# Threshold attention, then a GELU layer pair: the first batch's weights turned in TensorE's transpose mode, divided afterwards

## The chip, the cores and the metric

The kernel runs on one core of a Trainium2 chip. A core has a matrix engine (TensorE, PE in the profile), three engines for elementwise work (VectorE, DVE; ScalarE, ACT; GpSimd, POOL), a queue that only issues transfers (SyncE, SP) and 16 DMA engines. The engines run at the same time, each through its own list of instructions in order, and wait for each other by semaphores. The metric is the device time of one execution in microseconds; the lower, the better. Matmul results land in PSUM, small accumulation memory that TensorE writes and VectorE and ScalarE read; everything else lies in SBUF.

## What is computed

```python
# q, k, v: (8, 8, 576, 64) float32; tau = 0.02
scores = (q @ k.T) / sqrt(64)                       # per batch and head: 576 x 576
scores = where(scores >= max(scores, -1) - tau, scores, -1e9)
attn = exp(scores - max(scores, -1))
attn = attn / (sum(attn, -1) + 1e-9)
x = (attn @ v) -> (8 * 576, 8 * 64)                 # tokens x 512
h = x @ w_in                                        # 512 x 2048, float64 in memory
out = (0.5 * h * (1 + erf(h / sqrt(2)))) @ w_out    # 2048 x 512, float64 in memory
```

Eight batches of eight heads; then a feed-forward pair over all 4608 tokens. The matrix weights arrive as float64.

## The kernel before

**Work and its order.** The order of all instructions is written out by hand. Two heads make a pair (`p`), four pairs a batch (HP = 4), 32 pairs in all. A pair's 576 queries are cut into four chunks of 128 (two heads each) and one tail of 64 per head, both tails in one chunk: five steps (p, i). The main loop goes through steps, numbered n. In the first batch (p < EARLY = 4) n = 0 to 7 are the chunks 0 and 1 of the four pairs, n = 8 to 19 the chunks 2, 3 and the tail of each; from n = 20 on (BATCH) whole pairs follow one another. Each step issues, in this order: the scores (L403) and the head of the softmax (maximum L415 on VectorE, threshold L416 on GpSimd, exponential L418 on ScalarE); the product with v of an earlier step, where one is due; some work of the feed-forward blocks; the turning of the weights of the step before; the tail of the softmax (mask and sum, L434 on VectorE, then 1e-9 added to the sums, L437 on GpSimd).

**Turning.** The product with v needs the attention weights p with the keys on the partitions, so each 128 x 576 block of p is turned. From the second batch on VectorE turns blocks of 32 and DMA regroups them; x^T is then divided by the sums on GpSimd (`divide`, L545), with inverse sums that a DMA spreads over the partitions (`divisors`). In the first batch TensorE turns (`turn_p_early`, L335): `diagonal` (L440) takes the inverse of each query's sum on VectorE (L445) and ScalarE scales a 128 x 128 identity by it, for each of the two heads (L448); a matmul of p with that diagonal (L345) turns a block and divides it at once. A full step has ten: four blocks of 128 for each head, and two tails of 64 keys, one above the other. ScalarE copies the results out of PSUM (L353, L357, L364). In the first batch p is laid out so that the 64 tail keys of the first head and those of the second stand side by side.

**Product with v.** `weigh_v` (L506) makes x^T of a pair, 64 partitions for each head, and ScalarE copies it to its place in `xall` (L531), blocks of 256 tokens. In the first batch it is due after chunk 1 of a pair (tokens 0 to 255) and after its tail (256 to 575): `due` in the main loop.

**Weights.** The matrices come as 32 pieces of 128 x 512 float64. GpSimd's queue loads each twice, once as it is (L186) and once shifted by three bytes (L188); a generator `conversions` issues VectorE's and ScalarE's instructions that make float32 of them (L207, L208, L215, L217, L220), a few in each step, and each finished piece lets the next load go.

**Feed-forward.** 18 blocks of 256 tokens. The first eight are worked off between the attention steps, piece by piece: 64 matmuls of the first layer (L597), copies or gelus on ScalarE (L564, L570), 32 of the second (L612). `GOAL` says how many blocks are to be done by which step n; `goal` interpolates, `fill` issues what is owed. In the first batch the gelus are held back (the first layer's results are only copied, L564) and done together at n = 20 (`gelus_held`), because they need another function table than the exponentials (ACT_TABLE_LOAD). The last ten blocks follow in two groups of five after the attention, by a scheme with fewer products (L785, L667).

**PSUM.** Apart from the scores' two buffers, one pool of four banks (tag "mm") serves the turning (`tr`), x^T, the first layer (`hT`) and the second (`o_ps`). A bank is used again when its reader, mostly ScalarE, is done.

Of the kernel before, what the change touches and what calls it, by code (L numbers as in the profile page):

```python
# [18 lines left out]
def kernel(  # L19
# [40 lines left out]
    TAIL = S - MAIN  # L60
# [5 lines left out]
    TOK = 256  # L66
# [13 lines left out]
    ps = ctx.enter_context(tc.tile_pool(name="ps", bufs=4, space=PSUM))  # L80
# [12 lines left out]
    dg = late_end.enter_context(tc.tile_pool(name="dg", bufs=1))  # L93
    gp = late_end.enter_context(tc.tile_pool(name="gp", bufs=N_DF // 2 + 2))
    op = late_end.enter_context(tc.tile_pool(name="op", bufs=2))
# [25 lines left out]
    ident = const.tile([P, P], FP32, name="ident")  # L121
# [118 lines left out]
    st = {}  # L240
    x_blk = {}
# [93 lines left out]
    def turn_p_early(p, i):  # L335


        s = st[p]
        if i == 0 or (p < HP and i == 2):
            s["pT"] = [one.tile([P, KR, S], FP32, tag=f"pT{e}", name=f"pT{e}") for e in range(2)]  # L340
        w, diag = s.pop(("p", i)), s.pop(("diag", i))
        n = 1 if i == NC else 2

        def turn(to, cols, e):
            nc.tensor.matmul(to, lhsT=w[:, cols], rhs=diag[:, e, :], start=True, stop=True)  # L345

        for e in range(n):
            tr = ps.tile([P, NC, P], FP32, tag="mm", name="tr")
            for c in range(NC):
                at = e * (S + TAIL) + c * P  # L350
                turn(tr[:, c, :], slice(at, at + P), e)
            if i < NC:
                nc.scalar.copy(s["pT"][e][:, 0:NC, i * P:(i + 1) * P], tr)  # L353
        if i == NC:
            copy = nc.vector.tensor_copy if p == EARLY - 1 else nc.scalar.copy
            for e in range(2):
                copy(s["pT"][e][:, 0:NC, MAIN:S], tr[:, :, e * TAIL:(e + 1) * TAIL])  # L357
        tails = s["pT"][0][:, NC, :]
        tr = ps.tile([P, NC, P], FP32, tag="mm", name="tr")
        if i < NC:  # L360
            for e in range(2):
                at = MAIN + e * TAIL
                turn(tr[e * TAIL:(e + 1) * TAIL, 0, :], slice(at, at + TAIL), e)
            nc.scalar.copy(tails[:, i * P:(i + 1) * P], tr[:, 0, :])  # L364
            return
        turn(tr[0:TAIL, 0, :], slice(MAIN, S), 0)
        for e in range(2):
            rows = slice(e * TAIL, (e + 1) * TAIL)
            copy(tails[rows, MAIN:S], tr[0:TAIL, 0, rows])

    def scale_q(p):
        t = st[p]["q"]
# [64 lines left out]
            nc.gpsimd.tensor_scalar(pair[:, 0:n], pair[:, 0:n], 1e-9, None, op0=ALU.add)  # L437
            s["sum", i] = pair[:, 0:n]

    def diagonal(p, i):  # L440

        s = st[p]
        den = s.pop(("sum", i))
        n = den.shape[1]
        nc.vector.reciprocal(den, den)  # L445
        diag = s["diag", i] = dg.tile([P, 2, P], FP32, tag="inv", name="diag")
        for e in range(n):
            nc.scalar.activation(diag[:, e, :], ident, AF.Copy, bias=0.0, scale=den[:, e:e + 1])  # L448

    def divisors(p):  # L450

# [54 lines left out]
    def weigh_v(p, lo, hi):  # L506


        b, hp = divmod(p, HP)
        s = st[p]  # L510
        xT = ps.tile([P, 512], FP32, tag="mm", name="xT")
        for c in range(KR):
            for e in range(2):
                f = slice(e * D, (e + 1) * D)
                to = xT[f, 0:hi - lo]
                if p < EARLY:
                    rhs = s["pT"][0 if c == NC else e][:, c, lo:hi]
                else:
                    to = to.rearrange("p (g s) -> p g s", s=2 * Q)
                    rhs = by_64(s["pT"][e])[:, lo // (2 * Q):hi // (2 * Q), c, :]  # L520
                nc.tensor.matmul(  # L521
                    to, lhsT=s["v"][:, e, c, :], rhs=rhs, start=(c == 0), stop=(c == KR - 1))
        for n, o, at, size in in_blocks(b, lo, hi):
            if n not in x_blk:
                x_at[n] = x_slot(x_place(n))
                x_blk[n] = xall[:, x_at[n], :, :]
            to, x = x_blk[n][:, hp, o:o + size], xT[:, at - lo:at - lo + size]
            if p < EARLY and size == TOK:
                to = to.rearrange("q (p c) -> q c p", c=2)
                x = x.rearrange("q (c p) -> q c p", c=2)  # L530
            nc.scalar.copy(to, x)  # L531

    def in_blocks(b, lo, hi):
        while lo < hi:
            n, o = divmod(b * S + lo, TOK)
            size = min(TOK - o, hi - lo)
            yield n, o, lo, size
            lo += size
# [481 lines left out]
    BATCH = HP * SLOTS  # L1020
# [2 lines left out]
    DIVIDE = 3  # L1023
    START = 2 * HP + 2

    GOAL = [(-1, 0.0), (START - 1, 0.0), (BATCH - 1, 0.42)]
    GOAL += [(BATCH * (m + 2) + DIVIDE, x) for m, x in enumerate([1.92, 2.89, 3.86, 4.82, 5.79, 6.75])]
    GOAL += [(BATCH * B - 1, PLAIN - 0.44), (BATCH * B + 1, PLAIN - 0.17), (BATCH * B + WEIGH, PLAIN - 0.17)]

# [14 lines left out]
    for n in range(len(slots) + WEIGH + 1):  # L1044
        p, i = slots[n] if n < len(slots) else divmod(n, SLOTS)
        early = p < EARLY
        last = slots[n - 1] if 0 < n <= len(slots) else None
        if p < NP:
            scores(p, i)
            softmax_head(p, i)  # L1050
            if p < HP - 1 and i == 0:
                turn_qk_early(p + 1)
        elif n == len(slots):
            early_end.close()
            weights_first()
        gelus(0)
        if n == BATCH:
            gelus_held()
        table()
        for args in due:  # L1060
            weigh_v(*args)
        due = []
        if p > EARLY and i == WEIGH:
            for lo, hi in (0, WIDE), (WIDE, S):
                weigh_v(p - 1, lo, hi)
            if p == NP:
                divide(p - 1)
        owed += (goal(n) - goal(n - 1)) * BLK_NS * (PARTS[i] if not early and p < NP else 1.0)
        if early:
            fill(owed, tokens)  # L1070
            owed = 0.0
            table()
        if last and last[0] < EARLY and last[1] < NC:
            turn_p_early(*last)
        if early and n > 2:
            convert(0, 700 if i == NC else 1)
        if p < NP:
            softmax_tail(p, i)
        if p < NP and not early:
            turn_p(p, i)  # L1080
        if p < NP and not early:
            if i == 2:
                regroup(p, 1)
            if i > 2:
                regroup(p, i)
            if i == NC:
                divisors(p)
        if last and last[0] < EARLY and last[1] == NC:
            turn_p_early(*last)
        if p < 2 and i == 0:  # L1090
            load_piece()
            load_v_early(p + 2)
        if p == 1 and i == NC:
            load(HP)
        if n == BATCH - 3:
            load(HP + 1)
        if n == BATCH:
            for t in pd_tail + [turned_p[:, e, h, :, :] for e in range(2) for h in range(2)]:
                nc.gpsimd.memset(t[:, NB:4 * KR, :], 0.0)
        if EARLY < p < NP and i == DIVIDE:  # L1100
            divide(p - 1)
        if p >= HP and i == 1 and p + 2 < NP:
            loads = load_steps(p + 2)
        if p >= HP:
            next(loads, None)
        if p >= HP and i == 1 and p + 1 < NP or p == HP - 1 and i == 2:
            scale_q(p + 1)
        if p >= HP - 1 and i == 2 and p + 1 < NP:
            turn_qk(p + 1)
        convert(0 if n == 0 else 2000 if n < 3 else 3800 if n < BATCH - 1 else 1e9)  # L1110
        if early:
            diagonal(p, i)
        if not early:
            lag[0] = 2 if p < NP else 0
            fill(owed, tokens)
            owed = 0.0
        if last and last[0] < EARLY:
            if last[1] == 1:
                due.append((last[0], 0, TOK))
            if last[1] == NC:  # L1120
                due.append((last[0], TOK, S))
        if n == START - 1:
            tokens = TOK
        elif n == BATCH + 1:
            tokens = S
        elif p > EARLY and i == DIVIDE and p % HP == 0 or p == NP and i == WEIGH:
            tokens = p // HP * S
            leaving += [n for n in AWAY if n in x_blk and (n + 1) * TOK <= tokens]
        elif leaving and i < 2:
            put_away(leaving.pop(0))  # L1130
# [35 lines left out]
```

## Time and profile before

| | us |
|---|---|
| median of 4 runs | 1355.92 |
| lowest, highest | 1354.87, 1358.98 |
| the profiled execution, its own time | 1358.98 |
| its span, first to last instruction | 1357.2 |
| TensorE busy | 1334.6 |
| VectorE, ScalarE, GpSimd busy | 1063.3, 601.0, 633.4 |
| turning in the first batch, L345 (360 records) | 49.3 |
| the diagonals, L448 (36) | 12.6 |
| scores of n = 20 begin at | 141.84 |

TensorE's record of a matmul runs from its start to its modelled end, and these overlap, so sums of records are longer than the time they fill. Each float32 matmul leaves two records. In a timeline each row is a group of like instructions, with the idle time before it and what ended that in brackets. The clock row is the share of TensorE's full clock that was granted.

### The profile page before, as it was taken

Reading aid. Unit: us, or ns where it says so; the run is one execution under the profiler, and the core shown is the slowest. Engines: PE = TensorE matmul, PEld = TensorE weight load, DVE = VectorE, ACT = ScalarE, POOL = GpSimd, SP = SyncE. Lnnn points to the kernel's source line nnn. Section 1 sums busy time; section 2 is a strip of 40 time slices with the busy share of each in tenths; the row PEclk is TensorE's granted clock in tenths of the full one; section 3 lists DMA queues with packets and bytes.
Section 4 is the critical chain, followed back from the end, with each engine's and each line's share of the span. In section 5 each row is a group of like instructions: output and inputs, shape, how many; then the busy total and the mean of one; then the engine's idle time right before and its main releaser. Section 6 shows DMA issues by size and latency. Waiting matters only on the chain.

```text
span 1357.2 us, 20076 instructions
## 1 busy us (share of the span) xinstructions
PE 1334.6 (98%) x6398; PEld 905.6 (67%) x6398; DVE 1063.3 (78%) x2062; ACT 601.0 (44%) x1024; POOL 633.4 (47%) x1085
## 2 busy tenths in 40 slices
PE   9799999999999999999999999999999999999998
PEld 7577557557457557557547557568787787877877
DVE  6898777788888888888888888875658598385775
ACT  7666626537547538537637637513301112211120
POOL 5454354456456555554555552135363513625530
PEclk9899999999999999999999999999999999999999
DMA  9988267667777788787788777600000041000003
GB/s 293 295 292 271 57 150 164 134 159 177 167 170 181 164 188 186 155 210 178 154 196 186 156 170 161 124 9 1 0 1 0 5 120 32 1 1 0 1 0 78
DMA packets 212471, 169.18 MB, mean 125 GB/s; under 512 B 113872, under 2 KB 193600, under 8 KB 212368
## 3 DMA queue, kind: packets, MB, share of 16 engines
q1 hardware_dynamic: 188224, 112.53, 38.0%
q0 software_dynamic: 23712, 55.08, 13.2%
q8 instruction: 52, 0.85, 0.3%
q14 instruction: 51, 0.42, 0.1%
q10 hardware_dynamic: 432, 0.30, 0.1%
HBM read 72.73 MB, written 12.52 MB: 63 GB/s over the span
## 4 chain that ended last, share of the span: by engine, by line
PE 92%; DMA 3%; DVE 3%; ACT 1%; issue 0%; SPq 0%; POOL 0%; ACTq 0%; DVEq 0%
PE bank L785 34%; PE o_ps L612 17%; PE hT L597 16%; PE sc L403 13%; PE xT L521 10%; PE tr L345 2%; DMA v<-in_v_dram 1%; DMA x<-xall 1%; DMA xall<-in_moe_w_in_dram 1%; DVE nmx L415 1%; DVE p L434 1%; DMA k<-in_k_dram 0%; ACT p L418 0%; DVE power L217 0%; PE tr L315 0%
## 5 line engine op out<-in xcount | busy, mean ns | idle before, releaser
L418 ACT ACTIVATE p<-sc,nmx 128x576 f32<-128x576 f32 x288 | 201.6, 738 | 267.2 <-DVE nmx L415 266.7
L434 DVE SCALAR_TENSOR_TENSOR p<-sc,thr,p 128x576 f32<-128x576 f32 x288 | 225.2, 815 | 65.5 <-ACT p L418 62.4
L416 POOL TENSOR_SCALAR thr<-nmx,tau_eff 128x1 f32<-128x1 f32 x288 | 89.4, 311 | 379.1 <-DVE nmx L415 378.3
L415 DVE TENSOR_REDUCE nmx<-sc 128x1 f32<-128x576 f32 x288 | 205.2, 749 | 53.2 <-PE sc L403 52.2
L597 PE MATMUL hT<-xall,w_in 128*128 128x256 f32 x1024 | 241.9, 386 | 0.0
L612 PE MATMUL o_ps<-w_out,g 128*128 128x512 f32 x512 | 238.4, 606 | 0.0
L597 PEld LDWEIGHTS hT<-xall,w_in 128*128 128x128 f32 x1024 | 189.3, 190 | 51.0 <-issue 24.2
L667 DVE TENSOR_TENSOR c<-c,bank 128x320 f32<-128x320 f32 x304 | 146.9, 487 | 34.1 <-PE bank L785 20.7
L667 DVE TENSOR_TENSOR o<-o,bank 128x256 f32<-128x256 f32 x240 | 99.7, 419 | 93.7 <-PE bank L785 88.8
L612 PEld LDWEIGHTS o_ps<-w_out,g 128*128 128x128 f32 x512 | 93.7, 191 | 110.2 <-issue 107.8
L521 PE MATMUL xT<-pT,v 128*64 128x256 f32 (+1 forms) x1280 | 163.1, 409 | 0.0
L403 PE MATMUL sc<-kT,qT 64*128 64x288 f32 x960 | 158.4, 428 | 3.0 <-DVE p L434 2.4
L482 DVE STREAM_TRANSPOSE turned_p<-p 128x1152 f32<-128x1152 f32 x112 | 154.4, 1378 | 3.9
L403 PEld LDWEIGHTS sc<-kT,qT 64*128 64x128 f32 x960 | 90.9, 186 | 76.2 <-issue 63.2
L521 PEld LDWEIGHTS xT<-pT,v 128*64 128x64 f32 x1280 | 88.7, 137 | 72.0 <-issue 13.6
L785 PE MATMUL bank<-w_out,c 128*128 128x256 f32 x480 | 120.2, 381 | 0.5 <-DVE o L667 0.5
L265 POOL DMA_DIRECT2D v<-in_v_dram x208 | 110.9, 536 | 3.9 <-issue 1.9
L785 PEld LDWEIGHTS bank<-w_out,c 128*128 128x128 f32 x480 | 89.9, 190 | 18.8 <-DVE o L667 2.9
L838 ACT ACTIVATE c<-c 128x320 f32<-128x320 f32 (+1 forms) x80 | 46.9, 623 | 114.7 <-DVE c L667 114.6
L785 PE MATMUL bank<-t_out,c 128*128 128x256 f32 x320 | 82.7, 381 | 0.0
L785 PE MATMUL bank<-t_out,g 128*128 128x256 f32 x320 | 82.1, 379 | 0.0
L667 POOL TENSOR_TENSOR c<-c,g 128x320 f32<-128x320 f32 (+1 forms) x40 | 50.5, 1272 | 67.5 <-DVE c L667 67.5
(181 smaller groups left out, 1791.0 us busy)
## 6 DMA issues: line engine op xcount, KB each, us to landing
pT<-turned_p SPq DMA_DIRECT2D x448, 160.0 KB, 3.6
pT<-pd_tail SPq DMA_DIRECT2D x112, 80.0 KB, 3.1
q<-in_q_dram POOLq DMA_DIRECT2D x104, 72.0 KB, 3.4
k<-in_k_dram POOLq DMA_DIRECT2D x104, 72.0 KB, 3.3
inv<-turned SPq DMA_DIRECT2D x54, 128.0 KB, 4.0
v<-in_v_dram POOLq DMA_DIRECT2D x156, 40.0 KB, 3.2
out_dram<-o SPq DMA_DIRECT2D x40, 128.0 KB, 2.4
xall<-in_moe_w_out_dram POOLq DMA_DIRECT2D x9, 512.0 KB, 4.7
```

Of the source, the lines that this page charges most:

```text
L265: eng.dma_start(t[r:P:4, e, 0:n, :], rows[:, r * KR:r * KR + n, :])
L403: nc.tensor.matmul(sc[e][:, h, 0:HALF], lhsT=lhsT, rhs=s["kT"][rows, at:at + HALF], start=True, stop=True)
L415: nc.vector.tensor_reduce(nmx[:, e:e + 1], sc, axis=AXIS.XY, op=ALU.max, negate=True)
L416: nc.gpsimd.tensor_scalar(thr[:, e:e + 1], nmx[:, e:e + 1], -1.0, tau_eff, op0=ALU.mult, op1=ALU.subtract)
L418: nc.scalar.activation(w[:, e * S:(e + 1) * S].rearrange("p (h s) -> p h s", h=2), sc, AF.Exp, bias=nmx[:, e:e + 1], scale=1.0)
L434: nc.vector.scalar_tensor_tensor(row, sc[e][:, :, 0:HALF], thr[:, e:e + 1], row, op0=ALU.is_ge, op1=ALU.mult, accum_out=den[e])
L482: nc.vector.transpose(turned_p[:, :, i // 2, 0:NB, i % 2 * Q:(i % 2 + 1) * Q], w.rearrange("p (e b i) -> p e b i", e=2, i=Q))
L521: nc.tensor.matmul(to, lhsT=s["v"][:, e, c, :], rhs=rhs, start=(c == 0), stop=(c == KR - 1))
L597: nc.tensor.matmul(hT[:, j % 2, :], lhsT=w_in_sb[c][:, j * P:(j + 1) * P], rhs=x_blk[n][:, c, :], start=(c == 0), stop=(c == N_DM - 1))
L612: nc.tensor.matmul(o[:, 0:d_model], lhsT=g[j][:, m * P:(m + 1) * P], rhs=w_out_sb[j], start=(j == 0), stop=(j == N_DF - 1))
L667: eng.tensor_tensor(out, a, b, op=ALU.add)
L785: nc.tensor.matmul(to, lhsT=l, rhs=r, start=start and k == 0, stop=k == len(pairs) - 1, skip_group_check=not start)
```

## The change

The first batch's p is turned undivided, by `nc.tensor.transpose` with the plain identity, and x^T is divided instead. `turn_p_early` needs only p; the two tails of 64 become one block of 128 (in the last step of a pair, the last 128 columns are turned and the upper half of the result dropped). `diagonal` becomes `invert`, which only takes the inverse of the sums. The new `divide_early` follows each due `weigh_v`: matmuls with the inverse sums as the stationary operand, repeated over 64 columns, and the identity as the moving one spread them over 64 partitions for each head; ScalarE copies them to SBUF, and GpSimd multiplies x^T by them in place. And the goal at the end of the first batch rises from 0.42 to 0.5 blocks.

```diff
 def turn_p_early(p, i):
-    w, diag = s.pop(("p", i)), s.pop(("diag", i))
+    w = s.pop(("p", i))
     n = 1 if i == NC else 2
 
-    def turn(to, cols, e):
-        nc.tensor.matmul(to, lhsT=w[:, cols], rhs=diag[:, e, :], start=True, stop=True)
+    def turn(to, at):
+        nc.tensor.transpose(to, w[:, at:at + P], ident)
 
     for e in range(n):
         tr = ps.tile([P, NC, P], FP32, tag="mm", name="tr")
         for c in range(NC):
-            at = e * (S + TAIL) + c * P
-            turn(tr[:, c, :], slice(at, at + P), e)
+            turn(tr[:, c, :], e * (S + TAIL) + c * P)
...
     tr = ps.tile([P, NC, P], FP32, tag="mm", name="tr")
+    turn(tr[:, 0, :], MAIN if i < NC else S - P)
     if i < NC:
-        for e in range(2):
-            at = MAIN + e * TAIL
-            turn(tr[e * TAIL:(e + 1) * TAIL, 0, :], slice(at, at + TAIL), e)
         nc.scalar.copy(tails[:, i * P:(i + 1) * P], tr[:, 0, :])
         return
-    turn(tr[0:TAIL, 0, :], slice(MAIN, S), 0)
     for e in range(2):
         rows = slice(e * TAIL, (e + 1) * TAIL)
-        copy(tails[rows, MAIN:S], tr[0:TAIL, 0, rows])
+        copy(tails[rows, MAIN:S], tr[P - TAIL:P, 0, rows])
...
-def diagonal(p, i):
+def invert(p, i):
-    s = st[p]
-    den = s.pop(("sum", i))
-    n = den.shape[1]
+    den = st[p]["sum", i]
     nc.vector.reciprocal(den, den)
-    diag = s["diag", i] = dg.tile([P, 2, P], FP32, tag="inv", name="diag")
-    for e in range(n):
-        nc.scalar.activation(diag[:, e, :], ident, AF.Copy, bias=0.0, scale=den[:, e:e + 1])
+
+def divide_early(p, lo, hi):
+    s = st[p]
+    b, hp = divmod(p, HP)
+    tr = ps.tile([P, 512], FP32, tag="mm", name="tr")
+    for i in range(lo // P, -(-hi // P)):
+        den = s.pop(("sum", i))
+        to = tr[:, i * P - lo:min((i + 1) * P, hi) - lo]
+        for e in range(2):
+            one_of, cols = (den[:, e:e + 1], ident) if i < NC else (den, ident[:, e * TAIL:(e + 1) * TAIL])
+            nc.tensor.matmul(to[e * D:(e + 1) * D, :], lhsT=one_of.to_broadcast([P, D]), rhs=cols, start=True, stop=True)
+    by = dg.tile([P, S], FP32, tag="inv", name="inv")
+    nc.scalar.copy(by[:, 0:hi - lo], tr[:, 0:hi - lo])
+    for n, o, at, size in in_blocks(b, lo, hi):
+        x, y = x_blk[n][:, hp, o:o + size], by[:, at - lo:at - lo + size]
+        if size == TOK:
+            x = x.rearrange("q (p c) -> q c p", c=2)
+            y = y.rearrange("q (c p) -> q c p", c=2)
+        nc.gpsimd.tensor_tensor(x, x, y, op=ALU.mult)
...
-    GOAL = [(-1, 0.0), (START - 1, 0.0), (BATCH - 1, 0.42)]
+    GOAL = [(-1, 0.0), (START - 1, 0.0), (BATCH - 1, 0.5)]
...
         for args in due:
             weigh_v(*args)
+            divide_early(*args)
...
         if early:
-            diagonal(p, i)
+            invert(p, i)
```

More of the change, by code (lines that the diff above doesn't have):

```diff
@@ L438, in softmax_tail @@
             s["sum", i] = pair[:, 0:n]
-    def diagonal(p, i):
+    def invert(p, i):
+        den = st[p]["sum", i]
+        nc.vector.reciprocal(den, den)
+    def divide_early(p, lo, hi):
         s = st[p]
-        den = s.pop(("sum", i))
-        n = den.shape[1]
-        nc.vector.reciprocal(den, den)
-        diag = s["diag", i] = dg.tile([P, 2, P], FP32, tag="inv", name="diag")
-        for e in range(n):
-            nc.scalar.activation(diag[:, e, :], ident, AF.Copy, bias=0.0, scale=den[:, e:e + 1])
+        b, hp = divmod(p, HP)
[14 more added lines that the diff above has]
+            nc.gpsimd.tensor_tensor(x, x, y, op=ALU.mult)
     def divisors(p):
```

## The prediction

> **What bounds the kernel now.** The page first, its 40 slices of 34 us. The rows are TensorE, VectorE, the granted clock and the share of the DMA engines, in tenths.
>
> ```profile
> PE   9799999999999999999999999999999999999998
> DVE  6898777788888888888888888875658598385775
> PEclk9899999999999999999999999999999999999999
> DMA  9988267667777788787788777600000041000003
> ```
>
> From the fifth slice to the last but one TensorE is full. Only the first four (0 to 136 us, nearly all of the first batch, which alone the change touches) are different: DMA is at 8 or 9 and TensorE has a 7. So the second view is the busy time of that stage in stretches of 10 us (columns: the stretch, then PE, PEld, DVE, ACT, POOL, the clock, DMA share, GB/s).
>
> ```profile
> 40.00:50.00 10.00, 4.73 (x32) 3.76 (x31) 6.96 (x17) 5.33 (x12) 3.94 (x8) 0.89 1.05 336
> 70.00:80.00 10.00, 9.40 (x61) 7.41 (x61) 9.64 (x22) 6.76 (x14) 6.14 (x12) 1.00 0.90 330
> 100.00:110.00 10.00, 10.00 (x58) 6.94 (x57) 9.96 (x23) 7.14 (x17) 5.64 (x11) 1.00 0.99 306
> 110.00:120.00 10.00, 9.88 (x68) 8.18 (x67) 8.16 (x19) 6.38 (x15) 5.73 (x10) 1.00 1.08 301
> 130.00:140.00 10.00, 7.82 (x40) 6.52 (x39) 7.33 (x17) 7.27 (x16) 2.37 (x5) 0.83 0.31 112
> ```
>
> Three things are near full at once: DMA (the weights in 8-byte words, read twice), VectorE (their conversion, plus the softmax) and TensorE. Taking work from TensorE alone runs soon into the other two. Third view, the waits of 8 to 150 us: engine, line, releaser: total us, times, longest.
>
> ```profile
> PE tr L345 <- ACT diag L448: 8.0, 4, 5.3
> PE tr L345 <- ACT g L564: 2.2, 1, 2.2
> DVE nmx L415 <- PE sc L403: 7.3, 8, 2.6
> DVE power L207 <- DMA xall<-in_moe_w_in_dram: 2.8, 1, 2.8
> ```
>
> The 5.3 us are not the diagonal's own: it stands in ScalarE's queue behind L208, which waits for L207 on VectorE, which waits for a weight load. Last, TensorE's timeline (start, time, then the group) at three places, and ScalarE's at the end of the batch.
>
> ```profile
> 48.72 4.41 PE L345 MATMUL tr<-diag,p 128*128 128x128 f32 x20 [5.27 <-ACT diag L448]
> 98.47 1.24 PE L403 MATMUL sc<-pd_tail,qT 64*128 64x288 f32 x8
> 116.25 2.32 PE L345 MATMUL tr<-diag,p 128*128 128x128 f32 x20
> 118.50 1.24 PE L403 MATMUL sc<-pd_tail,qT 64*128 64x288 f32 x8
> 132.46 3.78 PE L345 MATMUL tr<-diag,p 128*128 128x128 f32 x20 [2.18 <-ACT g L564]
> 143.08 1.52 PE L345 MATMUL tr<-diag,p 128*128 128x128 f32 x10
> 144.53 4.58 PE L597 MATMUL hT<-xall,w_in 128*128 128x256 f32 x20
> 148.95 1.02 PE L612 MATMUL o_ps<-w_out,g 128*128 128x512 f32 x2
> ```
> ```profile
> 143.91 1.41 ACT L418 ACTIVATE p<-sc,nmx 128x576 f32<-128x576 f32 x2 [0.88 <-DVE nmx L415]
> 145.33 1.28 ACT L570 ACT_TABLE_LOAD   x1
> 146.63 3.23 ACT L570 ACTIVATE g<-g 128x512 f32<-128x512 f32 x6
> ```
>
> Each matmul leaves two records, so "x20" is ten. After waits of 5.27 and 2.18 us the same twenty take 4.41 and 3.78 us instead of 2.32: 2.0 and 1.5 us of slow clock.
>
> **The change, part by part.** *Turning p.* Now a full step has ten matmuls, 2.25 us from the start at 116.25 to the next at 118.50, so 112 ns a record and 225 ns a matmul. No row has a transpose-mode instruction. Dearest: two records like a matmul, 225 ns. Cheapest: the shortest pace of any record here, L325's 64x64 ones, eight from 20.26 to 20.64, 48 ns. I take one record with its weight load, 112 ns, since each record here comes with a load of 128 columns and those keep that pace. Nine for ten gives 1.01 us, 1.24 saved in 16 steps; in the four last steps of a pair 5 x 0.112 = 0.56 for 1.35 (101.90 to 103.25), 0.79 saved. Sum 23.0 us.
>
> *Inverse sums spread by TensorE.* Four matmuls after the first half of each pair, six after the second. The nearest row is L315, also 64 output columns: 32 records from 18.36 to 20.26, so 119 ns a matmul: 0.48 + 0.71, times four 4.8 us. If the 64-column halves did not overlap it would be 225 ns each, 9 us. TensorE is freed of 18.2 us (bounds -5 to 29).
>
> *ScalarE.* 36 diagonals leave (pairs take 0.69 us: 12.4 us). Eight copies come: 0.40 for 256 elements (L531), 0.44 for 320 (between that and 0.59 for 512, L353), 3.4 us. It stands at 6 to 7 of 10 there, so this buys no time itself; it only takes the diagonal out from between the softmax and the turning.
>
> *GpSimd.* Twelve multiplications by the nearest rows, L545: 0.74 for 256, 0.32 for 64; 7.2 us with the strided ones taken as plain (twice that at worst). Each waits for ScalarE's copy, which stands behind two exponentials. Behind it wait the sums' 1e-9 (L437) and the weight loads (L186, L188). In the step at 88 us: thresholds end 88.8, copies end 90.8, products 91.9, so loads leave some 1.5 us later than 91.43. VectorE waited only 0.7 us for loads after 50 us, so most of that is covered by earlier loads in flight; I charge 1.0 us in all, bounds 0 to 12 (8 times 1.5). The first feed-forward block needs divided x at 72.48; x is copied at 70.9, plus 0.36 and 0.74 is 72.0: just hidden.
>
> *More fill (0.42 to 0.5).* The order of instructions gives 64 instead of 54 first-layer matmuls before the first scores of the second batch, three more in every three steps, and equal counts again some 20 steps later. Ten are 4.42 us (144.53 to 148.95).
>
> *What becomes time, by stage.* 10 to 62 us: loads set the pace; only the turning at 48.72, no longer behind L208, lets the next scores start earlier; VectorE then waited 1.0 us: gain 1.0 (0 to 2.5). 62 to 83: VectorE at 9.6 of 10: 0. 83 to 130: three steps take 20.03 us (98.47 to 118.50) on TensorE; 23 transposes for 25 matmuls (6.03 us) save 3.45, spreading costs 0.71, fill 1.3: 18.6. But VectorE is busy 18.1 of 20 in those two rows and DMA's share is 0.99 and 1.08. VectorE is busy 42.1 of the 47 us from 83 to 130; of the 4.9 idle about 3 are behind TensorE or ScalarE; I take half of that, 1.5 (0 to 4.9). 130 to the scores at 141.84: the wait at 132.46 stays (it is for a PSUM bank that ScalarE frees only after the exponentials), then the turning after it takes 1.7 for 3.71 (nine of twenty records at that pace), the next 1.0 for 2.24, less 0.43 fill: 2.8, taken as 2.5 (0 to 4).
>
> *A new wait at the batch's end.* Before, ten first-layer matmuls run while ScalarE does exponentials, table load and gelus: scores end 143.08, second layer starts 148.95, 5.87 us later. Now none are left, and the second layer must wait for the first gelu: 146.63 + 0.62 = 147.25, 4.2 us after the scores, of which TensorE has work for 0.6. So of the 4.42 us moved only 5.87 - 4.2 = 1.7 is won, and a gap of 3.6 us may cost the slow clock (1.6): I take 0.9 (0 to 1.7). Behind it TensorE is full to the end, so the lead stays.
>
> Sum: 1.0 + 1.5 + 2.5 + 0.9 - 1.0 = 4.9. The profiled execution took 1358.98 us (span 1357.2, 1.8 around it), the highest of four; it would take 1354.1. Against the median 1355.92: **1351.0**.
>
> The Trainium skill speaks against the change ("TensorE: Matmul & The Clock Gate", Part 4): in a kernel a 128x128 transpose took some 275 ns, and the mode does not count as activity for the clock gate. By its 275 ns nine would be an estimated 2.5 us, dearer than now. But the present matmuls' own records also last 275 ns in the median while one follows another every 112 ns, so that figure is a duration, not a pace. That the clock ignores the mode, no run shows yet; by that rule the third rival below would be likelier.
>
> **Rivals.** *The loads and VectorE hold the first batch to its length.* For it: DMA shares of 0.97 to 1.09 in seven of the first twelve stretches. Against: 0.75 to 0.90 between 60 and 100. Then the first 130 us give nothing: 2.5 + 0.9 - 1.0 = 2.4, 1353.5.
>
> *Transposes are no quicker* (225 ns). Three steps become 20.03 - 0.45 + 0.71 + 1.3 = 21.6, 1.6 more, over 47 us 3.7 lost, the stage from 130 nothing: 1.0 - 3.7 + 0.9 - 1.0 = -2.8: 1358.7. For it: every row here has two records for a matmul. No row speaks against it, so it rests on the open price alone.
>
> *Slower: the clock.* Turning is 1.0 us instead of 2.25 and follows the scores at once, so TensorE's rest in a step of some 6.5 us becomes one gap instead of two. Waits of 1.95 us (62.86) cost no clock, of 2.18 did. Each costs 1.5 to 2.0 us on TensorE. From three such drops on in the filled steps from 75 us the gain is gone; with six, one in every second step and at the batch's end, it is 6 x 1.75 = 10.5: 1361.5. Against: in the filled steps TensorE has 18.6 of some 19.5 us of work.
>
> **How the numbers follow.** Forecast 0.42 (its own range 1346 to 1353), loads and VectorE 0.20, no quicker 0.13, clock 0.25. About 0.2% (2.7 us) can be told from no change. Faster (under 1353.2): 0.42 and half of the second case, 0.52. Slower (over 1358.6): the clock, and some of the third case, 0.30. Same 0.18. The range from 1344.5 (all bounds of the batch on the good side but transposes as taken) to 1361.5 takes in the cases.
>
> **What will show it.** One record a transpose, nine within 1.0 to 1.1 us; no wait for a diagonal; the second batch's first scores near 137 us instead of 141.84; a gap of 3 to 4 us before the first second-layer matmul; VectorE at 9 of 10 or more from 60 to 130. Two records, a clock row under 0.9 between 60 and 130, or weight loads that VectorE waits for by more than 3 us, would prove it wrong.

## The result, and the profile after

| | before | after |
|---|---|---|
| median, us | 1354.78 (66 runs) | 1357.42 (44 runs) |
| lowest, highest | 1352.11, 1358.98 | 1354.82, 1365.77 |
| ratio, 95% interval | | 1.0023, 1.0017 to 1.0029 |
| profiled execution, its span | 1358.98, 1357.2 | 1357.66, 1355.9 |
| turning in the first batch, records | 360 | 164 |

The changed kernel is slower by 0.23%, some 3 us; 4.9 us less was forecast. The two profiles alone would mislead: that of before was the highest of its 66 runs, so the changed kernel's looks 1.3 us shorter. A second profile of the kernel before, of an ordinary run (1354.88 us, b2_before below), is what the changed kernel is laid beside from here on.

First the 40 slices of the changed kernel (rows as before: TensorE, VectorE, clock, DMA).

```profile
PE   8798899999999999999999999999999999999998
DVE  7998677788888888888888888875758598385775
PEclk9899999999999999999999999999999999999999
DMA  9978267677778787787788677500000041000003
```

VectorE has gone from 8 to 9 in the second slice (34 to 68 us) and stays at 9 in the third; TensorE, at 9 before, has an 8 in the first, the fourth and the fifth. Next the stretches of 10 us of the changed kernel (PE, PEld, DVE, ACT, POOL, clock, DMA share, GB/s).

```profile
40.00:50.00 10.00, 6.40 (x32) 4.28 (x30) 9.83 (x23) 6.95 (x14) 6.69 (x13) 0.88 1.12 323
60.00:70.00 10.00, 8.11 (x44) 5.23 (x45) 9.96 (x24) 6.14 (x12) 3.43 (x8) 0.66 0.83 284
100.00:110.00 10.00, 9.96 (x65) 7.04 (x64) 9.97 (x23) 7.00 (x15) 5.30 (x10) 1.00 1.03 315
140.00:150.00 10.00, 5.94 (x20) 2.71 (x17) 6.37 (x14) 8.63 (x15) 1.34 (x8) 0.83 0.01 2
```

In the first three VectorE has next to no idle time left (0.17 us at most), while TensorE has 3.6 us of it from 40 and 1.9 us from 60. The last row is the new gap at the batch's end. The waits of the changed kernel from 8 to 150 us, of TensorE, VectorE and GpSimd (engine, line, releaser: total us, times, longest):

```profile
PE sc L399 <- DVE p L430: 10.6, 6, 3.2
PE o_ps L624 <- ACT g L582: 4.1, 1, 4.1
...
DVE power L207 <- DMA xall<-in_moe_w_out_dram: 2.5, 1, 2.5
DVE power L207 <- DMA turned_p<-in_moe_w_out_dram: 1.7, 1, 1.7
...
POOL xall L460 <- ACT inv L454: 11.7, 7, 3.1
```

Lines have moved: L399 are the scores (L403 before), L430 the masking that sums p (L434), L609 and L624 the two layers (L597, L612), L452, L454 and L460 the new matmuls, copies and multiplications. No wait for a diagonal is left. In its place the scores wait for VectorE's masking, which has to read a score bank before it can be written again: 10.6 us. In the ordinary run of before the same two waits read:

```profile
PE tr L345 <- ACT diag L448: 5.8, 2, 3.7
...
PE sc L403 <- DVE p L434: 0.3, 1, 0.3
```

So TensorE, freed of work, waits for VectorE 10.3 us longer, and no longer for diagonals. The same thing in one line for each kernel: the busy times from 8 us to the scores of n = 20, where the second batch begins (columns as in the stretches above). The ordinary run of before:

```profile
8.00:138.83 130.83, 120.96 (x862) 92.53 (x863) 117.87 (x260) 92.92 (x201) 61.33 (x118) 0.96 0.90 287
```

and the changed kernel:

```profile
8.00:139.62 131.62, 112.62 (x760) 81.49 (x760) 119.92 (x259) 84.36 (x173) 68.86 (x128) 0.95 0.88 285
```

TensorE's busy time fell by 8.3 us and ScalarE's by 8.6, though ten more first-layer matmuls are done in it. The batch did not get shorter (130.83 to 131.62), because VectorE is busy 90 and 91% of it and, with one instruction fewer, is busy 2.1 us longer.

TensorE's timeline of the changed kernel (start, time, group), in a filled step and at the batch's end, and ScalarE's there:

```profile
110.54 1.15 PE L345 MATMUL tr<-ident,p 128*128 128x128 f32 x9
111.52 1.14 PE L399 MATMUL sc<-pd_tail,q_tail 128*128 128x288 f32 x4
...
139.62 1.24 PE L399 MATMUL sc<-kT,qT 64*128 64x288 f32 x8
140.79 0.77 PE L345 MATMUL tr<-ident,p 128*128 128x128 f32 x5
145.62 6.25 PE L624 MATMUL o_ps<-w_out,g 128*128 128x512 f32 x10 [4.06 <-ACT g L582]
```
```profile
143.64 1.28 ACT L582 ACT_TABLE_LOAD   x1
144.93 4.27 ACT L582 ACTIVATE g<-g 128x512 f32<-128x512 f32 x8
```

Nine transposes are nine records and take 0.98 us (110.54 to 111.52), 109 ns each. At the end TensorE has nothing between the last transposes and the first gelu, 4.06 us.

### The profile page after: what moved, and what is told of

It is laid out like the page before. It is cut to its first block, busy times and chain, and to the rows that moved or that the text cites. A ratio compares the mean times of both kernels' runs of the same rounds, so it can differ in the third digit from the quotient of the medians.

```text
span 1355.9 us, 19803 instructions
## 1 busy us (share of the span) xinstructions
PE 1322.3 (98%) x6282; PEld 891.0 (66%) x6282; DVE 1065.9 (79%) x2062; ACT 590.5 (44%) x995; POOL 642.3 (47%) x1097
## 4 chain that ended last, share of the span: by engine, by line
PE 87%; DVE 1%; ACT 1%; DMA 1%; issue 0%; SPq 0%; POOL 0%; DVEq 0%; POOLq 0%; ACTq 0%
PE bank L797 34%; PE o_ps L624 16%; PE hT L609 15%; PE sc L399 12%; PE xT L533 10%; ACT p L414 0%; DVE nmx L411 0%; DVE p L430 0%; DMA x<-xall 0%; DMA turned<-turned 0%; ACT L582 0%; SPq L480 0%; SPq L482 0%; DVE power L217 0%; ACT g L576 0%
## 5 line engine op out<-in xcount | busy, mean ns | idle before, releaser
L430 DVE SCALAR_TENSOR_TENSOR p<-sc,thr,p 128x576 f32<-128x576 f32 x288 | 225.2, 815 | 65.7 <-ACT p L414 62.6
L609 PE MATMUL hT<-xall,w_in 128*128 128x256 f32 x1024 | 242.0, 386 | 1.8 <-ACT g L576 1.8
L624 PE MATMUL o_ps<-w_out,g 128*128 128x512 f32 x512 | 238.7, 606 | 4.1 <-ACT g L582 4.1
L609 PEld LDWEIGHTS hT<-xall,w_in 128*128 128x128 f32 x1024 | 189.3, 190 | 52.2 <-issue 23.0
L399 PE MATMUL sc<-kT,qT 64*128 64x288 f32 x960 | 161.2, 431 | 9.7 <-DVE p L430 9.1
L624 PEld LDWEIGHTS o_ps<-w_out,g 128*128 128x128 f32 x512 | 93.6, 191 | 114.1 <-issue 107.1
L533 PE MATMUL xT<-pT,v 128*64 128x256 f32 (+1 forms) x1280 | 167.5, 415 | 0.3
L399 PEld LDWEIGHTS sc<-kT,qT 64*128 64x128 f32 x960 | 91.9, 187 | 84.5 <-issue 71.7
```

The lines of the kernel that those rows point to most:

```text
L399: nc.tensor.matmul(sc[e][:, h, 0:HALF], lhsT=lhsT, rhs=s["kT"][rows, at:at + HALF], start=True, stop=True)
L430: nc.vector.scalar_tensor_tensor(row, sc[e][:, :, 0:HALF], thr[:, e:e + 1], row, op0=ALU.is_ge, op1=ALU.mult, accum_out=den[e])
L533: nc.tensor.matmul(to, lhsT=s["v"][:, e, c, :], rhs=rhs, start=(c == 0), stop=(c == KR - 1))
L609: nc.tensor.matmul(hT[:, j % 2, :], lhsT=w_in_sb[c][:, j * P:(j + 1) * P], rhs=x_blk[n][:, c, :], start=(c == 0), stop=(c == N_DM - 1))
L624: nc.tensor.matmul(o[:, 0:d_model], lhsT=g[j][:, m * P:(m + 1) * P], rhs=w_out_sb[j], start=(j == 0), stop=(j == N_DF - 1))
```

## The experiments

Ratios are to the kernel before, run on the same chip in the same session, with 95% intervals; each kernel has 4 to 12 runs. All diffs are against the changed kernel unless said.

### An ordinary run of before

No edit: the kernel before once more, for a profile of an ordinary run.

> The kernel before once more, for a second profile: the first fell on its slowest run (1358.98 of a median 1354.8). B: three or four windows of slow clock, clock 0.995 to 0.996, 1353 to 1356 us; against the first profile the lost 3 to 4 us should show up where that one had a window more.

1355.21 us (8 runs), ratio 0.9996 (0.9983 to 1.0008). The steps of the first batch, as the time between the first scores matmuls of the steps n named, in us; the last two columns are kernels that come below:

```
n           before  changed  turning alone  no products
0 to 7       39.45    39.36          38.93        38.87
7 to 12      32.63    34.90          32.52        32.42
12 to 18     40.07    41.21          39.56        40.35
18 to 20     18.20    15.84          14.36        15.83
20 to 41    124.80   125.02         125.00       125.91
0 to 41     255.15   256.33         250.37       253.38
```

Before, the scores of n = 7 began at 47.93 here and at 53.06 in the profile that the prediction read. The 5.27 us wait at 48.72 was therefore for the larger part a late load in one execution: here the same turning waits 2.16 us.

```profile
45.58 2.42 PE L345 MATMUL tr<-diag,p 128*128 128x128 f32 x20 [2.16 <-ACT diag L448]
```

The changed kernel loses 2.3 us from 7 to 12, where VectorE was full, loses 1.1 in the filled steps, and wins 2.4 us from 18 to 20 only. At n = 41 both kernels have issued the same feed-forward work, and the changed one is 1.2 us behind. By their spans these two executions differ by 2.8 us; where the other 1.8 us behind n = 41 come from is not shown, and the two profiles of the kernel before differ there by 1.1 us themselves.

### The goal of the fill

e1_goal42 puts the goal of the changed kernel back:

```diff
-    GOAL = [(-1, 0.0), (START - 1, 0.0), (BATCH - 1, 0.5)]
+    GOAL = [(-1, 0.0), (START - 1, 0.0), (BATCH - 1, 0.42)]
```

> The changed kernel with the fill goal back at 0.42 and all else kept. Theory A (the end of the batch: no first-layer matmuls are left to cover the gelus, so TensorE rests 4.1 us and then runs 3.4 us at the slow clock): the gap before the first second-layer matmul goes, 1352 to 1355 us, 3 to 5 below the changed kernel. Theory B (clock lost in the steps before, behind the shorter turning): the windows at 47 to 68 us stay, so 1356 to 1359, within 1.5 of the changed kernel. Theory C (GpSimd's divisions delay weight loads and VectorE): as B, and VectorE's load waits stay at about 4 us.

1358.60 us, 1.0023 (1.0013 to 1.0032): no different from the changed kernel, so theory A falls. e2_before_goal50 makes the opposite edit in the kernel before (0.42 to 0.5).

> The kernel before with the fill goal at 0.5 alone, diagonals kept. A: the same gap of 3 to 4 us opens before the second layer, and in the steps of 20 us three more first-layer matmuls (1.3 us) have no room on TensorE: 1357 to 1360 us. B and C: the goal is nearly neutral, 1354 to 1356.

1360.36 us, 1.0037 (1.0024 to 1.0050). The turning frees enough of TensorE that the moved fill no longer costs that, but with the division in the kernel it brings nothing either.

### The turning

e3_ident_matmul turns by plain matmuls with the identity, and the division stays on x:

```diff
-            nc.tensor.transpose(to, w[:, at:at + P], ident)
+            nc.tensor.matmul(to, lhsT=w[:, at:at + P], rhs=ident, start=True, stop=True)
```

> The changed kernel with plain matmuls by the identity in place of the transpose mode; the division stays on GpSimd. B (clock): each turning is 2.0 us again, TensorE rests less, the windows of slow clock fall back to the number of the kernel before: not slower than the changed kernel, 1354 to 1357 us. If TensorE's work is what counts: 23 us of transposes (by my forecast's price) come back in part, 1358 to 1362.

1362.96 us, 1.0058 (1.0041 to 1.0075). Its turning leaves 328 records, the transposes 164:

```profile
L345 PE MATMUL tr<-ident,p x328: 272/275/421, 13.5 to 147.4; 128*128 128x128 f32 x164
```

That makes the transposes worth 0.35% inside the changed kernel. They are not what made it slower. e6_mixed makes the edit of e3 for the first two steps of a pair (`if i < 2`) and keeps transposes in the others.

> The changed kernel with the transpose mode only for the chunks 2, 3 and the tails (steps 8 to 19); the chunks 0 and 1 (steps 0 to 7), where TensorE has time, are turned by matmuls with the plain identity, as in e3. B: the windows of slow clock near 47 and 61 us get fewer, clock 0.992 to 0.994, 1354 to 1356.5 us. If those steps are not where the clock is lost, or TensorE's work there counts: 1358 to 1361.

1359.32 us, 1.0032 (1.0019 to 1.0045), between the two: slower turning in the early steps of a pair helps nothing, whatever it does to TensorE's gaps.

e12_turn_alone has the transposes and nothing else of the change: no `divide_early(*args)`, and the goal of e1.

> The changed kernel with the division left out (x of the first batch stays undivided) and the fill goal put back to 0.42, so that only the turning differs from the kernel before. Theory bound (loads and VectorE hold the first batch to its length; the turning wins only what lies between 130 us and the batch's end): 2 to 2.5 us faster than before, ratio 0.9980 to 0.9986, as with goal 0.5. Rival, fill (the turning does win some 5 to 6 us and the moved fill gives it back at the batch's end): 5 us faster, 0.9960 to 0.9967. Rival, fill is needed: no faster than before.

1351.64 us, 0.9971 (0.9960 to 0.9981): 3.9 us faster than before, by the median more than "bound" allowed and less than "fill" asked for; the interval reaches into both. e14_turn_matmul is e12 with the edit of e3.

> As e12_turn_alone, with plain matmuls by the identity in place of transposes: no diagonal is waited for, but turning takes 2.25 us a step. Theory transposes (the gain is TensorE's shorter turning): the gain of e12_turn_alone is gone, ratio 0.999 to 1.001. Rival, wait (the gain is the missing wait for ScalarE's diagonals, 5.8 us in the typical run of before): the same as e12_turn_alone within 0.0007.

1353.54 us, 0.9988 (0.9977 to 0.9999): by the medians neither theory alone. Some 1.6 us of the 3.9 come from the diagonals that nobody waits for and from one matmul fewer a step, some 2.3 from the shorter turning; the intervals of the two overlap a little, so the split is not certain. The line of e12 from 8 us to the second batch:

```profile
8.00:133.44 125.44, 106.81 (x671) 74.00 (x671) 116.14 (x255) 81.58 (x164) 60.85 (x117) 0.93 0.93 299
```

TensorE's busy time is 14.2 us below before, the stretch 5.4 us shorter: VectorE's 116.14 us and 9.3 us of its idle time are what is left. TensorE waits for VectorE's masking here more than in the changed kernel, 13.3 us, in the fastest kernel of all: that wait marks room on TensorE and is not itself the loss.

### The division

e5_no_divide leaves out `divide_early(*args)`, at the new goal.

> The changed kernel without the division: no spreading matmuls, no copies of the inverse sums, no multiplications on GpSimd in the first batch, whose x therefore stays undivided. Theory C (the division holds up GpSimd's weight loads and slows VectorE): 1351 to 1354 us, 3 or more below the changed kernel's 1357.5. Theory B (slow clock in TensorE's gaps): the gaps only grow by the 4.8 us of spreading matmuls that leave, clock 0.990 to 0.991, 1355.5 to 1359.

1353.64 us, 0.9985 (0.9976 to 0.9993). So the division costs 0.38%, some 5 us, where turning and fill together win 2. Against e12 (0.9971) the moved fill would cost 1.9 us, but these intervals overlap. In the two profiles e5 is only 0.25 us later than e12 at n = 41 (0.9 us, counted from the first scores).

e8_no_mult keeps the spreading matmuls and ScalarE's copies and takes out the twelve multiplications:

```diff
-            nc.gpsimd.tensor_tensor(x, x, y, op=ALU.mult)
```

> The changed kernel with the spreading matmuls and ScalarE's copies kept and GpSimd's twelve multiplications left out (x of the first batch stays undivided). Theory GpSimd (the multiplications hold up GpSimd's queue of weight loads for up to 11.7 us of waits and make VectorE's conversions slower, 1.11 instead of 0.69 us): the time goes to that of the kernel without the whole division, 1353 to 1354.5 us beside a kernel before at 1355. Rival, the spreading matmuls (4.8 us of TensorE and a PSUM bank for ScalarE's copy): most of the division's 3.9 us stays, 1356.5 to 1357.5 us.

1354.87 us, 0.9995 (0.9984 to 1.0005). The multiplications are 3.8 us of the 5, well outside the intervals, spreading and copying the other 1.4, within them. VectorE's waits for loads hardly fell, from 4.4 us to 3.5:

```profile
DVE power L207 <- DMA xall<-in_moe_w_out_dram: 1.8, 2, 1.3
DVE power L207 <- DMA turned_p<-in_moe_w_in_dram: 1.5, 2, 1.2
```

So these waits are there without any products. To see whether they cost by their place in GpSimd's queue or by running at all, e9_late_mult issues them at the end of their step, behind the weight loads:

```diff
+            late_mult.append((x, y))
+
+    late_mult = []
+
+    def multiply():
+        while late_mult:
+            x, y = late_mult.pop(0)
             nc.gpsimd.tensor_tensor(x, x, y, op=ALU.mult)
...
         convert(0 if n == 0 else 2000 if n < 3 else 3800 if n < BATCH - 1 else 1e9)
+        multiply()
         if early:
```

> The changed kernel with the twelve multiplications issued at the end of their steps, behind the sums' 1e-9 and the step's weight loads in GpSimd's queue instead of ahead of them. Theory queue (what the division costs is that loads stand behind a multiplication that waits for ScalarE): 1354.5 to 1356 us, VectorE's waits for loads fall from 4.4 us to 2 to 3, and GpSimd no longer waits for ScalarE with a load behind. Rival, collision (VectorE's conversions are slower while GpSimd multiplies, wherever that stands): no gain, 1357 to 1358 us.

1358.37 us, 1.0020 (1.0011 to 1.0030). Nothing is won, though VectorE's waits for loads fell from 4.4 to 0.6 us: the queue theory falls. (TensorE waits once for a late product, 0.9 us, which is new.) e16_own_mult keeps e9's place, but GpSimd multiplies the copied inverse sums by themselves, and nobody reads them, so that x stays undivided (the diff is against e9):

```diff
-            late_mult.append((x, y))
+            late_mult.append(by[:, at - lo:at - lo + size])
...
-            x, y = late_mult.pop(0)
-            nc.gpsimd.tensor_tensor(x, x, y, op=ALU.mult)
+            x = late_mult.pop(0)
+            nc.gpsimd.tensor_tensor(x, x, x, op=ALU.mult)
```

> The changed kernel with x undivided and the twelve multiplications done by GpSimd on the copied inverse sums themselves, which nobody reads afterwards, behind the step's loads. Theory collision: as slow as the kernel with late products, ratio 1.0015 to 1.0025, with VectorE's conversions slower beside them. Rival, chain (the second layer's blocks and the loads wait for the products): as without products, 0.999 to 1.0005.

1356.39 us, 1.0008 (0.9995 to 1.0021), between the two expectations: some 1.8 us above e8 for GpSimd's work alone and some 1.6 below e9; no step is larger than its intervals. A product of one operand with itself is also a little shorter (eight of 256 elements: 757 ns in the mean, in e9 788). What the work does is in the lines from 8 us to the second batch. Without products (e8):

```profile
8.00:135.40 127.40, 111.93 (x759) 81.08 (x759) 116.35 (x258) 84.33 (x173) 59.81 (x118) 0.95 0.92 295
```

with idle products (e16):

```profile
8.00:137.15 129.15, 112.15 (x759) 81.20 (x760) 119.39 (x259) 84.38 (x173) 67.17 (x128) 0.95 0.89 290
```

and with late products (e9):

```profile
8.00:138.14 130.14, 111.58 (x761) 80.42 (x760) 121.30 (x259) 84.71 (x173) 67.51 (x128) 0.96 0.91 288
```

VectorE does the same work, 258 or 259 instructions, and is busy 3.0 to 5.0 us longer when GpSimd multiplies beside it; the stretch is 1.8 to 2.7 us longer. The single instructions show it as well. The conversion's last pass in the changed kernel (least, median and greatest ns):

```profile
L220 DVE SCALAR_TENSOR_TENSOR w_in<-w_in,power x16: 676/691/1115, 18.8 to 76.6; 128x512 f32<-128x512 uint32 x16
L220 DVE SCALAR_TENSOR_TENSOR w_out<-w_out,power x16: 670/692/1114, 83.1 to 140.3; 128x512 f32<-128x512 uint32 x16
```

and without products:

```profile
L220 DVE SCALAR_TENSOR_TENSOR w_in<-w_in,power x16: 670/692/695, 18.6 to 74.9; 128x512 f32<-128x512 uint32 x16
L220 DVE SCALAR_TENSOR_TENSOR w_out<-w_out,power x16: 672/691/693, 79.7 to 136.1; 128x512 f32<-128x512 uint32 x16
```

The median is the same; the few that fall beside a product take 1.1 us. Two products of the changed kernel, each with the VectorE pass that begins beside it:

```profile
41.19 0.74 POOL L460 TENSOR_TENSOR xall<-xall,inv 128x256 f32<-128x256 f32 x1 [0.43 <-ACT inv L454]
41.27 0.81 DVE L430 SCALAR_TENSOR_TENSOR p<-sc,thr,p 128x576 f32<-128x576 f32 x1
...
69.79 1.03 POOL L460 TENSOR_TENSOR xall<-xall,inv 128x256 f32<-128x256 f32 x1 [2.16 <-ACT inv L454]
70.26 1.11 DVE L220 SCALAR_TENSOR_TENSOR w_in<-w_in,power 128x512 f32<-128x512 uint32 x1
```

Beside the masking, which reads the scores in PSUM, neither is slowed (0.74 and 0.81 us, the usual times); beside the conversion both are. In the kernel with late products a pass of 0.42 us even takes 1.46:

```profile
L215 DVE TENSOR_SCALAR w_in<-xall x8: 407/417/1456, 17.7 to 72.7; 128x512 uint32<-128x512 uint32 x8
L215 DVE TENSOR_SCALAR w_out<-turned_p x7: 408/418/1460, 84.4 to 131.5; 128x512 uint32<-128x512 uint32 x7
```

Summed over the trace of the changed kernel, from 8 us to the second batch: the 20 VectorE instructions that overlap a product take 3.3 us longer than their like in e8 and e12, all others together 0.3 us longer. In e9 it is 14 instructions and 4.4 us, in e16 14 and 2.8. Nearly all of VectorE's longer busy time thus falls beside the products.

Two divisions without GpSimd. e13_dve_mult multiplies on VectorE straight from PSUM:

```diff
-        by = dg.tile([P, S], FP32, tag="inv", name="inv")
-        nc.scalar.copy(by[:, 0:hi - lo], tr[:, 0:hi - lo])
+        by = tr
...
-            nc.gpsimd.tensor_tensor(x, x, y, op=ALU.mult)
+            nc.vector.tensor_tensor(x, x, y, op=ALU.mult)
```

> The changed kernel with the twelve multiplications on VectorE, straight from the PSUM bank, so that neither GpSimd nor ScalarE's copy takes part. Theory collision (GpSimd's products slow VectorE's conversions): VectorE gains some 3 us back and pays some 4 (12 products of 0.3 to 0.4 us), in steps that it bounds: 1356.5 to 1358.5 us. Rival, chain of waits (ScalarE's copy and GpSimd's queue are what costs): 1354 to 1355.5 us.

1367.62 us, 1.0083 (1.0065 to 1.0102), dearer than either theory. Its VectorE waits:

```profile
DVE xall L459 <- ACT xall L542: 10.1, 6, 2.5
...
DVE xall L459 <- PE tr L452: 1.7, 1, 1.7
```

The products stand in VectorE's queue and wait 11.8 us for x and the spread sums, and everything of VectorE waits behind them. e17_scale_p divides p itself, on ScalarE, ahead of the transposes (no `divide_early`, goal 0.42):

```diff
-        den = st[p]["sum", i]
+        den, w = st[p].pop(("sum", i)), st[p]["p", i]
         nc.vector.reciprocal(den, den)
+        for e in range(den.shape[1]):
+            row = w[:, e * S:(e + 1) * S]
+            nc.scalar.activation(row, row, AF.Copy, bias=0.0, scale=den[:, e:e + 1])
```

> Transposes as in the changed kernel, goal 0.42, and the division done by ScalarE on p itself (36 activations of 128x576 by the inverse sum, in place, where the kernel before built 36 diagonals): no spreading, no GpSimd, no copy. ScalarE pays some 0.65 us for each (copies of 512 take 0.59) instead of 0.39, about 10 us more over the first batch, of which it idles 38 us in 132. Theory place (only the division through GpSimd and x is dear): 0.9975 to 0.999 of before, so faster than both kernels. Rival, wait (the transposes now stand behind 1.3 us of ScalarE a step, 0.6 us longer than behind the diagonals, and VectorE's maxima behind them): 0.9995 to 1.002.

1362.54 us, 1.0053 (1.0037 to 1.0069): slower than its rival allowed. One activation took 0.76 us, not 0.65; the transposes wait for it, and VectorE's masking waits for exponentials that stand behind it (0.9 us in the changed kernel):

```profile
PE tr L345 <- ACT p L442: 8.8, 8, 2.6
...
DVE p L430 <- ACT p L414: 11.6, 19, 1.3
```

None of the divisions tried is cheap enough to keep the gain of e12. The diagonals of the kernel before divide for 1.6 us (from e14 to before, 0.9988 to 1), with the product inside the turning; no version that divides beats the kernel before.

### The clock

Idle matmuls of identity by identity fill gaps, so that the granted clock stays up: e4_keep_on puts ten at the ends of steps 6, 8 and 11 and fifteen at the batch's end, e7_goal42_keep ten after 6 and 8 at goal 0.42, and e11_pad20 fifteen at the batch's end alone:

```diff
+    def keep_on(n):
+        pad = ps.tile([P, NC, P], FP32, tag="mm", name="pad")
+        for _ in range(n):
+            nc.tensor.matmul(pad[:, 0, :], lhsT=ident, rhs=ident, start=True, stop=True)
...
+        if n == BATCH:
+            keep_on(15)
```

> The changed kernel with idle matmuls of the identity by itself in four of TensorE's gaps: ten each (2.2 us) at the ends of steps 6, 8 and 11, fifteen (3.4 us) before the first second-layer matmul. They compute nothing that is read. B: the slow windows at 47, 61 and 146 us go, 3 of 5 windows at about 1.7 us each: 1352 to 1354 us, 4 to 5 below the changed kernel and below the kernel before. A without clock (the gap itself is the cost): 1357 to 1359, no gain. C: no gain.

1358.46 us, 1.0026 (1.0012 to 1.0041).

> The changed kernel with the goal at 0.42 and ten idle matmuls of the identity (2.2 us) at the ends of steps 6 and 8, where TensorE rests 3.2 us. At a clock of 0.994 the line through e1's runs gives 1353.8. B: clock 0.992 to 0.994, so 1354 to 1356. If the idle matmuls only take TensorE's time, as e4's 1358.5 at a clock of 0.995 may mean: 1358 to 1360.

1358.89 us, 1.0026 (1.0015 to 1.0037).

> The changed kernel with 15 idle 128x128 matmuls (identity by identity, about 3.4 us) in the one gap of 4.1 us ahead of the second layer at the batch's end. Theory gap clock (the ten matmuls after the gap take 6.25 us instead of 4.56 us): 1.7 us are won, 1355.5 to 1356 us, and ten matmuls take 4.5 us. Rival (the clock there costs nothing in the end, or the idle matmuls push the work behind them): 1357 to 1358.5 us.

1357.59 us, 1.0013 (1.0001 to 1.0024). The five matmuls (ten records) after the gap did get the clock:

```profile
142.51 3.51 PE L370 MATMUL pad<-ident 128*128 128x128 f32 x30
146.73 4.56 PE L629 MATMUL o_ps<-w_out,g 128*128 128x512 f32 x10 [0.71 <-ACT g L587]
151.22 1.24 PE L404 MATMUL sc<-kT,qT 64*128 64x288 f32 x8
```

They take 4.56 us instead of 6.25. By ratio 1.4 us may be won, but the interval overlaps that of the changed kernel. In the early steps the idle matmuls won nothing: e4's mean clock over its runs was 0.9953, the changed kernel's 0.9911, and e4 was no faster. They take TensorE's time too, so what the clock alone is worth there stays open. That it is not what made the changed kernel slower shows in e12: its mean clock is 0.9911 as well, and it is 3.9 us faster than before.

## Why the prediction was wrong

**Turning** was right in its cost: one record, 109 ns where 112 were taken, no wait for a diagonal. In the kernel it wins 3.9 us alone (e12). The stages were forecast at 1.0, 0, 1.5 and 2.5 us; the table gives turning alone 0.5 (0 to 7), 0.1 (7 to 12), 0.5 (12 to 18) and 3.8 (18 to 20). The first term rested mostly on a late load in the profiled execution. The third and fourth together, 4.0, came out as 4.3. But they were forecast for the whole change, and with the division and the fill in the kernel the same four stages give 0.1, -2.3, -1.1 and 2.4. That VectorE leaves little of the 23 us was right: 14.2 us less of TensorE's busy time became 5.4 us in that profile and 3.9 in the medians.

**GpSimd** is the step that failed. It was charged "1.0 us in all, bounds 0 to 12", for weight loads held up in its queue. GpSimd did stand 11.7 us for ScalarE's copies, and VectorE waited 4.4 us for loads, which passed the 3 us that the prediction named as its refutation. But that mark could not tell: the profile that the prediction read has 3.7 us of such waits, e8 without products 3.5, and with them down to 0.6 us (e9) nothing was won. What was put at nothing is that GpSimd's products slow VectorE's conversions, while VectorE, busy 91% of the stage, has little idle time to take it up: 3 to 5 us more of VectorE's busy time for the same instructions. The products cost 3.8 us by ratio (e8 to the changed kernel). That this lies inside the bounds is luck; they were made for another cost. e16 points to the work alone as part of it; how the rest divides into slowed instructions and the wait for the divided x is not settled.

**Spreading** was priced at 4.8 us of TensorE and nothing on the path but 0.71 in three filled steps. By the ratios it takes 1.4 us of time with ScalarE's copies (e5 to e8), but these intervals overlap. The division as a whole, charged 1.0 us, costs 5.1 us at the new goal (e5 to the changed kernel) and 7.0 at the old one (e12 to e1), both clear of their intervals.

**The moved fill** was to win 0.9 us, half of the slow clock's price having been taken off. Its gap is 4.06 us, forecast 3.6, and it does bring the slow clock in full: 6.25 us for 4.56. Together this eats the 4.4 us that were moved. From 20 to 41 the changed kernel takes 125.02 us, before 124.80, with ten matmuls fewer left to do. What the fill is worth depends on the rest: putting the goal back changes nothing in the changed kernel (e1), raising it costs 1.9 us without the division (e12 to e5, within the intervals) and 5.0 in the kernel before (e2).

The terms as measured by ratio: turning -3.9, moved fill +1.9, spreading +1.4, products +3.8, in all +3.2 us; the changed kernel is 1.0023 of before, +3.1. That they add up is no evidence, since each is the step from one kernel to the next; in another order the fill is worth nothing and the division 7.0. The first and last are well told from nothing, the two between only as a sum of 3.3.

**The marks named ahead:** one record, yes; nine within 1.0 to 1.1 us, yes (0.98); no diagonal, yes; the second batch's scores at 137, no (139.62); a gap of 3 to 4 us, yes (4.06); VectorE at 9 of 10 from 60 to 130, in the mean (9.01), but only in three of the seven rows. Two of the three refutations came: the loads, and a clock of 0.66 from 60 to 70 us. The second shows no cause: the ordinary run of before has 0.77 in the same 10 us, and keeping the clock up there won nothing.

**The rivals.** "Loads and VectorE hold the first batch" named the right engine, but not that its own work would grow. "Transposes no quicker" falls with e3. "The clock" had the right sign and about twice the size (1361.5, so 5.6 us slower; measured are some 3) by a mechanism that e4 and e7 do not bear out and that e12's clock speaks against. Nor is there a border between waits of 1.95 and 2.18 us: in the changed kernel TensorE waited 2.68 us until 82.57, and the clock from 82.5 to 84.5 us stayed at 1.00.

**The base.** The sum was made against an execution at 1358.98 us, which held a late load that the ordinary run does not have; the term of 1.0 us in the 4.9 rested mostly on it, and turning alone won 0.5 us there.

## What to carry to other kernels

Ask of each engine that a change gives work to whether it runs beside the engine that sets the stage's length, and price the slowing of that one, not only the queue behind the new instruction. Work taken from an engine that waits for another wins only a part of its time: here 14.2 us of TensorE gave 3.9, with VectorE busy 90% of the stage. Before a wait of a single profile is counted as a gain, a second profile of the same kernel should show it too.

## What the runs showed of the hardware

- A VectorE pass of 128x512 over SBUF that takes 0.69 us alone took up to 1.11 us beside a GpSimd multiplication of 128x256 in the changed kernel, one of 0.42 us up to 1.46 (e9), and the multiplication up to 1.30 us instead of 0.74. The masking, which reads PSUM, kept its 0.81 us beside one, and so did the multiplication its 0.74.
- A float32 128x128 transpose is one record and follows the last after 109 ns; the matmul by the identity is two records and 233 ns (e3, nine from 76.58 to the scores at 78.68 us). Records of both have a median of 273 to 275 ns, so a record's length says nothing of the pace.
- Within one kernel the time falls with the mean granted clock (44 runs of the changed kernel: correlation -0.79, some 1.0 us for 0.001), yet idle matmuls that raised the clock by 0.004 did not shorten it. Between kernels it does not hold: e12 and the changed kernel have the same mean clock, 0.9911, and lie 0.5% apart. Lower clock and longer time within a kernel may have a common origin in the gaps of the early steps; that was not shown.
